# Float64 weight decoding without its maximum and mask, and a new step list, in a fused linear-attention and two-layer mixture kernel

## The chip, the cores and the metric

The kernel runs on one core of one Trainium2 chip. The metric is the time of one execution in microseconds (us), as the device reports it. Engines are named as in the profile: PE is TensorE's matmuls and PEld its weight loads, DVE is VectorE, ACT is ScalarE, POOL is GpSimd, SP is SyncE, which issues the DMAs.

## The reference

Three blocks follow each other. The first is a linear attention with a decaying state over 768 positions (4 batches, 8 heads of 48). The second is a feed-forward layer `g = h * cos(h)` with `h = x @ w_in`, whose two matrices `w_in` (384 x 2048) and `w_out` (2048 x 384) arrive as float64. The third is a soft mixture of eight experts.

```python
for t in range(S):
    cur = np.einsum('bhd,bhe->bhde', u[None] * kt, vt)
    y[:, :, t] = np.einsum('bhd,bhde->bhe', rt, state + cur)
    state = wt[:, :, :, None] * state + np.einsum('bhd,bhe->bhde', kt, vt)
...
h = x @ w_in
g = h * np.cos(h)
return (g @ w_out).astype(np.float32)
...
logits = x @ phi          # softmax over tokens (dispatch) and over slots (combine)
slot_out[e] = np.maximum(slot_input[e] @ w1[e], 0.0) @ w2[e]
return (c @ slot_out).astype(np.float32)
```

## The kernel before

The 3072 tokens are cut into 24 blocks of 128 (j, or t in the feed-forward part). Every piece of work is a named step, and a string `HEAD` of about 1900 step names is the whole schedule: the steps are emitted in that order, and each engine executes its own instructions in that order. There is no other scheduler; an engine that waits holds up everything behind it in its own list.

The steps that matter here:

- Attention for block j: loads `lw lk lr lv lz`, transposes on TensorE `wT rT kT kN`, two scans on VectorE `scan` (line 149) and `sp` (line 157), `ks` (line 184, it reads the transposed k out of PSUM), `L`, `mask`, `z`, `st`, `bo`; `ru` and `D` are POOL's (lines 162, 163, 207); matmuls `A U y`; the result x is split into a high and a low part by `xh` and `xl`.
- Decoding the float64 weights, 256 columns of `w_in` (i.0 to i.7) or 256 rows of `w_out` (o.0 to o.7) at a time. `raw` loads the pairs of 32-bit words. `abs` (line 325, ScalarE) reads the high word as a float32 and takes its absolute value. `mx` (line 329, VectorE) takes the maximum with the smallest high word that still fits float32. `d1` (line 333) shifts left by 3 and masks, `d2a` (line 338) brings sign and top exponent bit in from the high word, `d2b` (line 346) brings three bits in from the low word. For w_in, `whi`, `wn`, `wc` then split the result into a high and a low part on ScalarE and TensorE; for w_out, `oT`, `oc`, `om`, `pc`, `pT`, `ps` multiply it with phi ahead of time. The raw tiles of most blocks have two buffers, so a `raw` waits for the `d2b` of two blocks before.
- Feed-forward for block t and quarter q of the columns: `h.t.q` is nine matmuls (lines 434 to 436), then `turns` (ScalarE), `rest` (VectorE), `cos` (ScalarE), `mul` (VectorE), `gT` (TensorE), `gc` (ScalarE), `l` (TensorE).
- Once per pair of blocks g the logits are summed up: `sum lc max exp xt xr xd dT dc ltok E es`, between TensorE, VectorE and ScalarE.

The decoding is spread over the first quarter of the list, between attention blocks 0 to 5 and feed-forward blocks 0 and 1. Block i.0 is decoded in two halves, so 16 blocks make 17 of each decode step.

Of the kernel before, what the change touches and what calls it, by code (L numbers as in the profile page):

```python
# [21 lines left out]
def rwkv_moe_kernel(ctx: ExitStack, tc: tile.TileContext, r, k, v, w, u, w_in, w_out, phi, w1, w2, cst, out):  # L22
    nc = tc.nc
# [323 lines left out]

    def e_d2s(x, n, hf=None):

        lo = part(raw_t[x, n, hf], hf)[..., 0]  # L350
        nc.vector.tensor_scalar(out=lo, in0=lo, scalar1=29, scalar2=None, op0=ALU.logical_shift_right)

    def e_d2p(x, n, hf=None):
        ai, dst = cut(x, n, hf)
        nc.gpsimd.tensor_tensor(out=dst, in0=part(raw_t[x, n, hf], hf)[..., 0], in1=ai, op=ALU.add)
# [529 lines left out]
d2b.o.3 lz.1 mx.o.1 wc.0.1 abs.o.0 U.1 rz.1.0 st.1.0 d1.o.1 kT.2 mx.o.0 d2a.o.1 z.1.1 raw.i.4 d2b.o.1 ks.2 d1.o.0 y.0 lw.3 st.1.1 abs.o.2 rz.1.1 sr.2
d2a.o.0 lk.3 mx.o.2 kN.2 ksn.2 d2b.o.0 d1.o.2 oT.3 z.2.0 oT.0 d2a.o.2 abs.i.1 lr.2 mx.i.1 oc.0 d2b.o.2 y.1 oc.3 xh.0 d1.i.1 oT.2 xl.0 xh.1 abs.i.4
xl.1 oT.4 oc.2 oT.5 oc.4 lr.3 oc.5 ru.2 wT.3 oT.1 sp.2 wf.3 rT.2 oc.1 lv.2 d2a.i.1 mx.i.4 lw.4 d2b.i.1 U.2 L.2 st.2.0 d1.i.4 raw.i.3 whi.1 scan.3 bo.2
om.0 wn.1.0 d2a.i.4 rz.2.0 wn.1.1 wc.1.0 z.2.1 wc.1.1 lw.5 abs.i.3 bs.2 d2b.i.4 whi.4 A.2 raw.i.6 h.0.0 D.2 ru.3 mx.i.3 lr.4 kT.3 sr.3 d1.i.3 st.2.1
d2a.i.3 pc.0 mask.2 turns.0.0 d2b.i.3 raw.i.5 wn.4.0 whi.3 sp.3 ks.3 wc.4.0 wn.4.1 rest.0.0 lz.2 abs.i.6 wc.4.1 wT.4 mx.i.6 wf.4 z.3.0 cos.0.0 oT.6
d1.i.6 oc.6 scan.4 wn.3.0 wn.3.1 wc.3.0 oT.7 abs.i.5 d2a.i.6 rT.3 h.1.0 sr.4 d2b.i.6 oc.7 wc.3.1 mx.i.5 L.3 d1.i.5 whi.6 turns.1.0 mul.0.0 wn.6.1  # L890
rest.1.0 wn.6.0 wT.5 wc.6.1 gT.0.0 raw.i.7 rz.3.0 pT.0 d2a.i.5 h.0.1 rz.2.1 lr.5 sp.4 ps.0 lk.4 lv.3 A.3 wc.6.0 bo.3 y.2 abs.i.7 bs.3 D.3 gc.0.0 wf.5
d2b.i.5 whi.5 raw.o.4 turns.0.1 lw.6 om.1 mx.i.7 mask.3 xh.2 kN.3 wn.5.0 cos.1.0 ksn.3 rest.0.1 cos.0.1 xl.2 pc.1 d1.i.7 mul.1.0 d2a.i.7 wc.5.0 wn.5.1
kT.4 wc.5.1 abs.o.4 U.3 ks.4 d2b.i.7 mx.o.4 h.0.2 turns.0.2 lw.7 st.3.0 lk.5 mul.0.1 whi.7 d1.o.4 kN.4 h.1.1 ru.4 wn.7.0 gT.0.1 z.3.1 rest.0.2 lz.3
lv.4 rz.3.1 ksn.4 wn.7.1 turns.1.1 d2a.o.4 scan.5 st.3.1 cos.0.2 d2b.o.4 y.3 wc.7.0 raw.o.5 abs.o.5 wc.7.1 bo.4 mul.0.2 rest.1.1 l.0.0 mx.o.5 rT.4
pT.1 cos.1.1 gc.0.1 h.0.3 ps.1 oT.9 L.4 raw.o.6 d1.o.5 gT.0.2 mul.1.1 lv.5 lr.6 lk.6 bs.4 d2a.o.5 turns.0.3 rest.0.3 xh.3 oT.8 abs.o.6 gc.0.2 oc.8
h.1.2 d2b.o.5 oT.11 mx.o.6 z.4.0 oc.9 xl.3 cos.0.3 turns.1.2 oT.10 oc.11 d1.o.6 l.0.1 mul.0.3 A.4 oc.10 raw.o.7 U.4 lz.4 d2a.o.6 om.2 st.4.0 d2b.o.6
abs.o.7 kT.5 gT.0.3 gc.0.3 rest.1.2 z.4.1 ru.5 h.1.3 ks.5 mx.o.7 pc.2 pT.2 st.4.1 cos.1.2 ps.2 oT.12 d1.o.7 sr.5 mul.1.2 bo.5 gT.1.1 ru.6 rT.5 sp.5
d2a.o.7 oc.12 l.0.2 L.5 bs.5 wT.6 rz.4.1 d2b.o.7 close D.4 wf.6 h.2.0 gc.1.1 kN.5 mask.4 gT.1.0 turns.1.3 ksn.5 gc.1.0 oT.13 A.5 oc.13 oT.15 rest.1.3
gT.1.2 oT.14 z.5.0 l.1.0 rz.4.0 D.5 oc.15 turns.2.0 mask.5 oc.14 y.4 lk.7 l.1.1 om.3 cos.1.3 xh.4 mul.1.3 rest.2.0 lz.5 U.5 xl.4 h.2.1 pc.3 st.5.0
lw.8 gc.1.2 z.5.1 cos.2.0 mul.2.0 scan.6 turns.2.1 gT.1.3 pT.3 sr.6 rest.2.1 bo.6 ps.3 rz.5.1 gc.1.3 h.2.2 kT.6 gT.2.0 l.1.2 l.0.3 l.1.3 cos.2.1 sp.6  # L900
rT.6 lr.7 ks.6 turns.2.2 wT.7 gc.2.0 sum.0 st.5.1 rest.2.2 lc.0 mul.2.1 bs.6 cos.2.2 L.6 kN.6 lv.7 lk.8 rz.5.0 h.2.3 ksn.6 A.6 mul.2.2 D.6 wf.7 max.0
exp.0 lv.6 U.6 z.6.0 turns.2.3 gT.2.1 scan.7 gc.2.1 xt.0 rest.2.3 st.6.0 lr.8 z.6.1 st.6.1 xr.0 h.3.0 sr.7 cos.2.3 lv.8 kT.7 turns.3.0 mul.2.3 ru.7
gT.2.2 gc.2.2 xd.0 bo.7 ks.7 rT.7 bs.7 dT.0 ltok.0 h.3.2 lz.6 rest.3.0 kN.7 l.2.0 dc.0 cos.3.0 ru.8 ksn.7 lr.9 sp.7 mul.3.0 rz.6.1 lw.9 E.0.0 y.5
mask.6 turns.3.2 xh.5 h.3.1 gT.2.3 turns.3.1 wT.8 l.2.1 L.7 bo.8 l.2.2 rest.3.2 E.0.1 lk.9 xl.5 wf.8 cos.3.2 rest.3.1 gc.2.3 mul.3.2 rz.6.0 bs.8 A.7
cos.3.1 es.0 gT.3.0 h.3.3 gc.3.0 scan.8 sr.8 kT.8 turns.3.3 lk.10 mul.3.1 gT.3.2 l.2.3 rest.3.3 l.3.0 y.6 D.7 gc.3.2 h.4.1 gT.3.1 cos.3.3 turns.4.1
mask.7 ks.8 xh.6 rT.8 z.7.0 mul.3.3 sp.8 xl.6 wT.9 rest.4.1 h.4.0 rz.7.0 wf.9 L.8 gc.3.1 turns.4.0 gT.3.3 U.7 D.8 cos.4.1 lz.7 lw.10 st.7.0 z.7.1 A.8
mul.4.1 gc.3.3 l.3.1 rest.4.0 lr.10 l.3.2 rz.7.1 cos.4.0 st.7.1 scan.9 l.3.3 y.7 sum.1 mask.8 h.4.2 mul.4.0 turns.4.2 sr.9 rest.4.2 gT.4.1 sp.9 ru.10
lc.1 cos.4.2 max.1 kN.8 mul.4.2 lw.11 gc.4.1 ksn.8 h.5.0 wT.10 bo.10 exp.1 xt.1 gT.4.0 wf.10 kT.9 h.4.3 bs.10 ks.9 xr.1 xd.1 xh.7 dT.1 turns.5.0 kN.9
gc.4.0 gT.4.2 rest.5.0 dc.1 turns.4.3 xl.7 U.8 cos.5.0 gc.4.2 l.4.0 ltok.1 z.8.0 rest.4.3 mul.5.0 l.4.1 st.8.0 E.1.0 z.8.1 ru.9 h.5.1 st.8.1 rT.9
cos.4.3 mul.4.3 scan.10 turns.5.1 gT.4.3 rest.5.1 h.5.2 L.9 rz.8.1 z.9.0 ksn.9 cos.5.1 gc.4.3 lw.12 lz.8 turns.5.2 lv.9 mul.5.1 A.9 U.9 rest.5.2  # L910
cos.5.2 bo.9 lv.10 h.6.1 sr.10 st.9.0 rz.8.0 gT.5.1 mul.5.2 wT.11 turns.6.1 gc.5.1 h.5.3 sp.10 lz.9 rest.6.1 z.9.1 st.9.1 kT.10 bs.9 wf.11 D.9 gT.5.0
turns.5.3 E.1.1 cos.6.1 l.4.2 y.8 gc.5.0 xh.8 l.5.0 scan.11 l.4.3 rest.5.3 mask.9 rT.10 mul.6.1 ks.10 sr.11 cos.5.3 mul.5.3 gT.5.2 kN.10 h.6.0 gc.5.2
# [109 lines left out]
```

## Time and profile before

| what | value |
|---|---|
| time, median of 3 runs | 530.23 us (529.28 to 530.65) |
| the profiled execution's own time | 529.87 us |
| its span, first to last instruction | 528.2 us |
| PE busy | 486.2 us (92%) |
| DVE busy | 434.1 us (82%) |
| ACT busy | 319.4 us (60%) |
| POOL busy | 100.0 us (19%) |

The profiled execution lies within the range of the timed ones. Its span is 1.67 us shorter than its time; that difference lies outside the first and last instruction. A busy share is an average over the whole span: the first 64 us, the middle and the last 50 us have different limits.

### The profile page before, as it was taken

The numbers are of one execution on the slowest core, as the hardware profiler recorded it, in microseconds if no ns is written. First come the engines' busy times: TensorE is split into PE (matmuls) and PEld (weight loads), VectorE is DVE, ScalarE is ACT, GpSimd is POOL, SyncE is SP. The second block draws the span as 40 slices with busy tenths as digits, with TensorE's granted clock in tenths as the row PEclk, the third lists the DMA queues.
The fourth block names the chain that finished last, engine by engine and source line by source line (L and its number), as shares of the span: only waits on it lengthen the run. The fifth ranks groups of instructions, "written<-read, shape, count | busy, mean of one in ns | idle before, by whom it ended". The sixth has DMA issues, their size and how long they took to land.

```text
span 528.2 us, 15546 instructions
## 1 busy us (share of the span) xinstructions
PE 486.2 (92%) x6515; PEld 381.2 (72%) x6515; DVE 434.1 (82%) x826; ACT 319.4 (60%) x703; POOL 100.0 (19%) x127
## 2 busy tenths in 40 slices
...
GB/s 184 331 208 70 190 143 203 178 58 70 54 77 64 13 80 88 62 47 59 78 23 56 76 31 51 58 91 82 57 2 47 337 378 7 118 269 325 402 175 267
DMA packets 146325, 67.47 MB, mean 128 GB/s; under 512 B 127184, under 2 KB 134352, under 8 KB 146256
## 3 DMA queue, kind: packets, MB, share of 16 engines
...
## 4 chain that ended last, share of the span: by engine, by line
PE 70%; DVE 18%; ACT 4%; DMA 4%; issue 2%; SPq 0%; ACTq 0%; DVEq 0%
PE h L434 11%; PE h L436 10%; PE h L435 10%; PE gT L468 7%; PE l L483 4%; PE E L579 4%; PE y L267 4%; PE A L193 3%; PE U L239 2%; PE hps L767 2%; DVE lt L214 2%; PE so L807 2%; PE wT L134 2%; PE kT L134 2%; PE kN L200 1%
## 5 line engine op out<-in xcount | busy, mean ns | idle before, releaser
L434 PE MATMUL h<-wu,x 128*128 128x512 f32 x288 | 121.6, 422 | 0.8 <-DVE g L461 0.8
L436 PE MATMUL h<-wu,x 128*128 128x512 f32 x288 | 113.1, 393 | 0.0
L435 PE MATMUL h<-wu,x 128*128 128x512 f32 x288 | 112.5, 391 | 0.0
L449 ACT ACTIVATE g<-h 128x512 int32<-128x512 f32 (+1 forms) x96 | 57.1, 596 | 54.4 <-PE h L436 47.2
L457 ACT ACTIVATE g<-g,half_pi 128x512 f32<-128x512 f32 (+1 forms) x97 | 69.0, 718 | 22.7 <-DVE g L453 21.5
L461 DVE TENSOR_TENSOR g<-g,h 128x512 f32<-128x512 f32 x96 | 64.5, 675 | 17.2 <-ACT g L457 16.9
L453 DVE SCALAR_TENSOR_TENSOR g<-g,h 128x512 f32<-128x512 int32 (+1 forms) x96 | 64.6, 675 | 12.2 <-ACT g L449 11.7
L207 POOL TENSOR_SCALAR_AFFINE_SELECT lt<-bo 64x512 f32<-64x512 f32 x48 | 35.3, 736 | 179.6 <-ACT bo L230 121.3
L434 PEld LDWEIGHTS h<-wu,x 128*128 128x128 f32 x288 | 54.2, 188 | 15.0 <-DVE g L461 4.1
L474 ACT COPY gt<-gT 128x512 f32<-128x512 f32 x89 | 51.8, 583 | 20.0 <-PE gT L468 15.6
L436 PEld LDWEIGHTS h<-wu,x 128*128 128x128 f32 x288 | 54.0, 188 | 12.4
L435 PEld LDWEIGHTS h<-wu,x 128*128 128x128 f32 x288 | 54.4, 189 | 8.7
L468 PE MATMUL gT<-cs,g 128*128 128x128 f32 x384 | 57.7, 275 | 0.6 <-ACT gt L474 0.5
L162 POOL TENSOR_TENSOR ru<-rn,u_b 128x384 f32<-128x384 f32 x24 | 28.9, 1203 | 137.5 <-DVE bo L225 70.3
L468 PEld LDWEIGHTS gT<-cs,g 128*128 128x128 f32 x384 | 44.7, 141 | 8.3 <-issue 2.2
L214 DVE COPY_PREDICATED lt<-cs,A 64x512 f32<-64x512 uint32 x48 | 35.4, 737 | 3.2 <-PE A L193 1.8
L149 DVE TENSOR_TENSOR_SCAN qt<-wf,one_b 128x520 f32<-128x520 f32 x24 | 30.9, 1289 | 5.5 <-ACT wf L144 5.3
L253 ACT COPY rzs<-z 64x192 f32<-64x192 f32 x96 | 33.4, 348 | 1.8 <-DVE z L248 0.9
L483 PE MATMUL l<-gt,p_sb 128*32 128x128 f32 x768 | 31.7, 277 | 1.9 <-ACT gt L474 1.6
L178 DVE TENSOR_TENSOR lt<-rT,pt 64x512 f32<-64x512 f32 x48 | 32.8, 684 | 0.5
L157 DVE TENSOR_TENSOR_SCAN pt<-wf,ini_f 128x520 f32<-128x520 f32 x24 | 30.6, 1274 | 0.1
L267 PEld LDWEIGHTS y<-lt,rzs 128*32 128x32 f32 x1536 | 24.7, 112 | 6.3 <-issue 2.4
...
## 6 DMA issues: line engine op xcount, KB each, us to landing
...
```

The lines of the kernel that those rows point to most:

```text
L214: nc.vector.copy_predicated(out=lt[j % 2][h, a], mask=mask[h].bitcast(U32).unsqueeze(1).to_broadcast([64, NS, C]), data=ps[h])
L267: nc.tensor.matmul(ps[m:m + 32, o, c * C:(c + 1) * C], lhsT=rz[:, c, p, a, 32 * b:32 * b + 32], rhs=L[:, a, 2 * p + c, :], start=m not in ...
L434: nc.tensor.matmul(half[:, f], lhsT=xh[:, c, :], rhs=wh, start=(c == 0), stop=False)
L435: nc.tensor.matmul(half[:, f], lhsT=xl[:, c, :], rhs=wh, start=False, stop=False)
L436: nc.tensor.matmul(half[:, f], lhsT=xh[:, c, :], rhs=wl, start=False, stop=(c == KD - 1))
L449: nc.scalar.activation(gt.bitcast(I32), hp, AF.Copy, bias=0.25, scale=1.0 / TWO_PI)
L453: nc.vector.scalar_tensor_tensor(out=gt, in0=gt.bitcast(I32), scalar=-TWO_PI, in1=hp, op0=ALU.mult, op1=ALU.add)
L457: nc.scalar.activation(gt, gt, AF.Sin, bias=half_pi[:, 0:1])
L461: nc.vector.tensor_tensor(out=gt, in0=gt, in1=hp, op=ALU.mult)
L468: nc.tensor.transpose(ps[:, m * 128:(m + 1) * 128], gt[:, m * 128:(m + 1) * 128], ident)
L474: (nc.vector.tensor_copy if n >= ATT and n % 8 in (1, 2, 5) else nc.scalar.copy)(gt_t[t, q], pend.pop(("gT", t, q)))
L483: nc.tensor.matmul(lps_t[g][32 * m:32 * m + 32, o:o + TB], lhsT=p_sb[:, 4 * q + m, :], rhs=gt[:, m * 128:(m + 1) * 128], start=first, stop ...
```

## The change

ScalarE's `abs` gets a scale of 2^-112, which lowers the exponent so far that what follows needs no maximum and no mask. The `mx` step is gone, `d1` only shifts, `d2a` takes the sign bit alone from the high word. Three steps that no list used go as well. `HEAD` is replaced by another list of the same steps without the 17 `mx`.

```diff
-        nc.scalar.activation(part(a_t[x, n], hf), part(raw_t[x, n, hf], hf)[..., 1].bitcast(F32), AF.Abs)
-
-    def e_mx(x, n, hf=None, eng=nc.vector):
-        a = part(a_t[x, n], hf)
-        eng.tensor_scalar(out=a, in0=a, scalar1=TINY_HI_F, scalar2=None, op0=ALU.max)
-
-    def e_d1(x, n, hf=None):
+        nc.scalar.activation(part(a_t[x, n], hf), part(raw_t[x, n, hf], hf)[..., 1].bitcast(F32), AF.Abs, scale=2.0 ** -112)
+
+    def e_shift(x, n, hf=None):
         ai = part(a_t[x, n].bitcast(I32), hf)
-        nc.vector.tensor_scalar(out=ai, in0=ai, scalar1=3, scalar2=0x3FFFFFF8, op0=ALU.logical_shift_left, op1=ALU.bitwise_and)
-
-    def e_d2a(x, n, hf=None):
+        nc.vector.tensor_scalar(out=ai, in0=ai, scalar1=3, scalar2=None, op0=ALU.logical_shift_left)
+
+    def e_sign(x, n, hf=None):
 
         hi, ai = part(raw_t[x, n, hf], hf)[..., 1], part(a_t[x, n].bitcast(I32), hf)
-        nc.vector.scalar_tensor_tensor(out=ai, in0=hi, scalar=-0x40000000, in1=ai, op0=ALU.bitwise_and, op1=ALU.bitwise_or)
+        nc.vector.scalar_tensor_tensor(out=ai, in0=hi, scalar=-0x80000000, in1=ai, op0=ALU.bitwise_and, op1=ALU.bitwise_or)
...
-raw.i.0.1 d2a.i.2 d2b.i.2 L.0 bo.0 bs.0 whi.2 U.0 D.0 scan.1 st.0.0 A.0 rz.0.0 sr.1 raw.i.0.0 kT.1 z.0.1 abs.i.0.1 mask.0 abs.i.0.0 ks.1 ru.1 wn.2.1
...
-TINY_HI_F = 2.0 ** (0x38000000 // 0x800000 - 127)
```

What the new list does is best seen where VectorE comes to `ks.3`, about 63 us into the program of before. Before, VectorE's rows there are these (ai_644 is block i.3, ai_722 is block i.6, ks_711 is `ks.3`, pt_709 is `sp.3`):

```order
L329 TENSOR_SCALAR ai_644<-ai_644 128x768
L153 RECIPROCAL ini_f<-qt_613 128x8
L333 TENSOR_SCALAR ai_644<-ai_644 128x768
L256 TENSOR_TENSOR st_state<-U_1_589,z_1_640 128x192
L338 SCALAR_TENSOR_TENSOR ai_644<-rawi_610,ai_644 128x768
L214 COPY_PREDICATED lt_125<-cs,A_651 64x512 x2
L346 SCALAR_TENSOR_TENSOR ai_644<-rawi_610,ai_644 128x768
L157 SCALAR_TENSOR_TENSOR pt_709<-wf,ini_f 128x520
L184 TENSOR_TENSOR ks_711<-kT_687,qt_613 128x512
```

In the change the same place on VectorE reads as follows (ai_661 is block i.3, ai_712 is block i.6, ks_717 is `ks.3`, pt_724 is `sp.3`; lines 334 and 342 are the old 338 and 346, and line 329 is now the shift):

```order
L214 COPY_PREDICATED lt_125<-cs,A_644 64x512 x2
L334 SCALAR_TENSOR_TENSOR ai_661<-rawi_601,ai_661 128x768
L342 SCALAR_TENSOR_TENSOR ai_661<-rawi_601,ai_661 128x768
L153 RECIPROCAL ini_f<-qt_642 128x8
L184 TENSOR_TENSOR ks_717<-kT_694,qt_642 128x512
L157 SCALAR_TENSOR_TENSOR pt_724<-wf,ini_f 128x520
L329 TENSOR_SCALAR ai_712<-ai_712 128x768
```

The maximum of block i.3 is gone, and the scan `sp.3` has moved from ahead of `ks.3` to behind it.

The second place is the start of SP's list. Before, the loads come in this order (wn_121, kn_119 and rn_117 are w, k and r of block 0, wn_122 is w of block 1, rawi_156 is weight block i.2):

```order
L117 DMA wn_121<-in_w_dram 128x8x48
L310 DMA rawi_156<-in_moe_w_in_dram 128x3x512
L117 DMA kn_119<-in_k_dram 128x8x48
L662 DMA u_b<-in_u_dram 128x384
L663 DMA phi_sb<-in_moe_phi_dram 128x3x32
L117 DMA rn_117<-in_r_dram 128x8x48
L117 DMA wn_122<-in_w_dram 128x8x48
```

In the change SP's list begins so (rawi_157 is block i.2, rawi_175 the first half of block i.0):

```order
L117 DMA wn_121<-in_w_dram 128x8x48
L117 DMA kn_119<-in_k_dram 128x8x48
L310 DMA rawi_157<-in_moe_w_in_dram 128x3x512
L117 DMA wn_122<-in_w_dram 128x8x48
L310 DMA rawi_175<-in_moe_w_in_dram 128x3x256
L117 DMA rn_117<-in_r_dram 128x8x48
L649 DMA u_b<-in_u_dram 128x384
```

The k of block 0 now goes ahead of the first weight block, and r of block 0 behind the first half of i.0.

## Rows read from the trace of the kernel before

**Rows 1.** First line of the page.

```profile
span 528.2 us, 15546 instructions
```

**Rows 2.** Busy time in five stretches: start:end, length, engines, PE clock, DMA share, GB/s.

```profile
6.32:28.00 21.68, 12.63 (x102) 8.32 (x102) 20.59 (x31) 7.89 (x18) 7.95 (x8) 0.85 1.07 277
28.00:64.10 36.10, 25.48 (x346) 18.73 (x345) 34.96 (x54) 19.53 (x38) 8.46 (x6) 0.78 0.65 146
64.10:114.10 50.00, 48.34 (x585) 38.46 (x589) 47.43 (x77) 36.85 (x79) 12.31 (x12) 0.95 0.72 162
114.10:476.60 362.50, 358.16 (x4858) 287.24 (x4846) 311.65 (x618) 235.96 (x523) 61.30 (x70) 1.00 0.38 89
476.60:528.20 51.60, 40.46 (x637) 27.77 (x637) 19.24 (x48) 16.81 (x45) 6.67 (x10) 0.95 0.82 289
```

**Rows 3.** The chain that ended last, share of the span by engine.

```profile
PE 70%; DVE 18%; ACT 4%; DMA 4%; issue 2%; SPq 0%; ACTq 0%; DVEq 0%
```

**Rows 4.** That chain in order of time, 20 to 70 us: start, length, what.

```profile
20.94 1.08 DVE ai L329 x2
...
34.53 0.47 DVE ao L329
...
50.52 4.71 DMA rawi<-in_moe_w_in_dram
...
55.31 0.94 ACT ai L325
...
56.27 0.56 DVE ai L329
...
62.40 1.15 DVE pt L157
...
64.19 1.12 PE wT L134 x4
...
69.14 0.46 PE woT L388 x3
```

**Rows 5.** VectorE's decode groups to 115 us, shapes apart: count, busy us, mean ns.

```profile
L338 DVE SCALAR_TENSOR_TENSOR ai<-rawi,ai 128x768 int32<-128x768 int32 x7 | 8.6, 1225 | 0.0
...
L329 DVE TENSOR_SCALAR ao<-ao 128x768 f32<-128x768 f32 x8 | 4.4, 552 | 1.3 <-ACT ao L325 1.3
L333 DVE TENSOR_SCALAR ao<-ao 128x768 int32<-128x768 int32 x8 | 4.4, 548 | 0.0
L329 DVE TENSOR_SCALAR ai<-ai 128x768 f32<-128x768 f32 x7 | 4.3, 619 | 1.0 <-ACT ai L325 0.9
...
L329 DVE TENSOR_SCALAR ai<-ai 128x384 f32<-128x384 f32 x2 | 1.2, 612 | 0.0
```

**Rows 6.** VectorE's timeline: start, length, line, what.

```profile
9.11 0.56 DVE L329 TENSOR_SCALAR ai<-ai 128x768 f32<-128x768 f32 x1
...
28.00 0.56 DVE L329 TENSOR_SCALAR ao<-ao 128x768 f32<-128x768 f32 x1
28.48 0.55 DVE L346 SCALAR_TENSOR_TENSOR ai<-rawi,ai 128x384 int32<-128x384 int32 x1
...
57.94 2.10 DVE L338 SCALAR_TENSOR_TENSOR ai<-rawi,ai 128x768 int32<-128x768 int32 x1
```

**Rows 7.** POOL's timeline around 58 us.

```profile
58.24 0.99 POOL L162 TENSOR_TENSOR ru<-rn,u_b 128x384 f32<-128x384 f32 x1
59.31 1.60 POOL L163 TENSOR_TENSOR ru<-ru,kn 128x384 f32<-128x384 f32 x1
```

**Rows 8.** Two ScalarE groups to 115 us: with scale and bias, and a plain copy.

```profile
L449 ACT ACTIVATE g<-h 128x512 int32<-128x512 f32 x9 | 5.4, 601 | 3.9 <-PE h L436 3.9
L382 ACT CAST wu<-wl 128x512 fp32r<-128x512 f32 x8 | 4.7, 585 | 9.4 <-PE wl L377 9.4
```

**Rows 9.** The chain in order of time, one hand-off of the logits.

```profile
459.59 0.45 PE lc L496 x2
...
465.32 1.07 PE E L579 x8
```

More of the change, by code (lines that the diff above doesn't have):

```diff
@@ L346, in e_d2b @@
         nc.vector.scalar_tensor_tensor(out=dst, in0=part(raw_t[x, n, hf], hf)[..., 0], scalar=29, in1=ai, op0=ALU.logical_shift_right, op1=ALU.bitwise_or)
[L348 to L355, printed above, removed]
     def win(n):
@@ L885 @@
[L885 to L912, printed above, removed]
@@ L969 @@
-rest.23.3.0 l.22.0 mul.23.3.1 gc.23.0 l.22.1 gT.22.2 rest.23.1 cos.23.1 cos.23.3.0 we.6 gc.22.2 gT.23.2 l.23.0 l.22.2 mul.23.1 gc.23.2 l.22.3 gT.23.1
-mul.23.3.0 gc.23.1 gT.23.3 l.23.1 gc.23.3 l.23.2 l.23.3 sum.11 lc.11 we.7 E.10.1 tab max.11 quart.11 exp.11 dT.11 es.10 dc.11 E.11.1 E.11.0 esl.11.1
-ltok.11 esl.11.0
+lw.0 lk.0 raw.i.2 z.0.0 wT.0 lw.1 kT.0 wf.0 scan.0 raw.i.0.0 abs.i.2 ks.0 sr.0 sp.0 d1.i.2 d2a.i.2 wT.1 lr.0 misc kN.0 ru.0 wf.1 scan.1 ksn.0 d2b.i.2
+rT.0 lv.0 abs.i.0.0 lr.1 raw.i.0.1 lk.1 abs.i.0.1 sr.1 U.0 L.0 d1.i.0.0 raw.o.2 lw.2 rT.1 raw.o.0 lv.1 bo.0 lk.2 bs.0 D.0 sp.1 lz.0 st.0.0 d2a.i.0.0
@@ new lines @@
+z.0.1 A.0 L.1 raw.i.1 mask.0 st.0.1 whi.2 rz.0.1 wn.2.0 ru.1 d1.i.0.1 kT.1 lr.2 wn.2.1 z.1.0 wc.2.0 d2a.i.0.1 d2b.i.0.0 abs.o.3 rz.0.0 d2b.i.0.1 bo.1
+wT.2 lz.1 ks.1 d1.o.3 wf.2 kN.1 lw.3 ksn.1 bs.1 d2a.o.3 wc.2.1 raw.i.4 D.1 scan.2 A.1 d2b.o.3 whi.0 mask.1 wn.0.0 abs.o.1 lv.2 d1.o.1 U.1 d2a.o.1
+wc.0.0 st.1.0 wn.0.1 d2b.o.1 z.1.1 abs.o.0 abs.o.2 rz.1.0 y.0 d1.o.0 st.1.1 wc.0.1 d2a.o.0 sr.2 oT.2 ru.2 oc.2 oT.3 xh.0 oc.3 d2b.o.0 rz.1.1 kT.2
+d1.o.2 xl.0 oT.1 ks.2 lv.3 oT.0 sp.2 y.1 abs.i.1 oc.1 d2a.o.2 d1.i.1 oc.0 kN.2 d2b.o.2 wT.3 om.0 wf.3 xh.1 d2a.i.1 xl.1 oT.4 ksn.2 oT.5 oc.4 U.2
@@ new lines @@
+d2b.i.1 oc.5 z.2.0 raw.i.3 st.2.0 lw.5 whi.1 abs.i.4 z.2.1 bo.2 rT.2 bs.2 st.2.1 L.2 wn.1.0 wc.1.0 lz.3 d1.i.4 wn.1.1 wc.1.1 d2a.i.4 rz.2.0 oT.7
+scan.3 A.2 abs.i.3 d2b.i.4 d1.i.3 lk.3 D.2 mask.2 d2a.i.3 raw.i.6 h.0.0 oc.7 whi.4 wn.4.1 d2b.i.3 rz.2.1 wc.4.1 kT.3 turns.0.0 wn.4.0 lw.4 whi.3 lr.3
+pc.0 ru.3 abs.i.6 sr.3 raw.i.5 ks.3 wc.4.0 oT.6 sp.3 oc.6 d1.i.6 wn.3.0 rest.0.0 wc.3.0 wn.3.1 lk.4 d2a.i.6 rT.3 wT.4 d2b.i.6 wc.3.1 L.3 z.3.0 wf.4
+whi.6 cos.0.0 h.1.0 abs.i.5 scan.4 pT.0 raw.i.7 turns.1.0 wn.6.1 d1.i.5 wc.6.1 wn.6.0 bo.3 wT.5 mul.0.0 wc.6.0 sr.4 d2a.i.5 h.0.1 abs.i.7 d2b.i.5 sp.4
@@ new lines @@
+whi.5 bs.3 lz.2 A.3 ps.0 turns.0.1 lr.4 rz.3.0 y.2 wf.5 D.3 xh.2 om.1 rest.1.0 d1.i.7 kN.3 cos.1.0 mask.3 ksn.3 wn.5.0 rest.0.1 cos.0.1 wc.5.0 wn.5.1
+mul.1.0 raw.o.4 gT.0.0 wc.5.1 d2a.i.7 kT.4 xl.2 lz.4 d2b.i.7 mul.0.1 abs.o.4 whi.7 U.3 pc.1 ks.4 ru.4 raw.o.5 st.3.0 h.0.2 wn.7.0 d1.o.4 turns.0.2
+z.3.1 gc.0.0 d2a.o.4 wn.7.1 rest.0.2 wc.7.1 st.3.1 h.1.1 rT.4 gT.0.1 cos.0.2 abs.o.5 wc.7.0 scan.5 turns.1.1 d2b.o.4 bo.4 lw.6 oT.8 oc.8 mul.0.2
+rest.1.1 sr.5 kN.4 d1.o.5 h.0.3 bs.4 cos.1.1 L.4 mul.1.1 pT.1 rz.3.1 d2a.o.5 lk.5 ksn.4 gc.0.1 y.3 turns.0.3 h.1.2 rest.0.3 oT.9 xh.3 ps.1 cos.0.3
@@ new lines @@
+raw.o.7 lv.4 d2b.o.5 oT.11 gT.0.2 z.4.0 turns.1.2 oc.11 lr.5 oc.9 D.4 xl.3 oT.10 oc.10 A.4 rest.1.2 U.4 mul.0.3 l.0.0 sp.5 l.0.1 st.4.0 mask.4 abs.o.7
+lw.7 lr.6 z.4.1 om.2 cos.1.2 pc.2 gc.0.2 raw.o.6 mul.1.2 abs.o.6 h.2.0 ru.5 gT.0.3 rz.4.1 rT.5 gc.0.3 pT.2 d1.o.6 h.1.3 ps.2 rz.4.0 d1.o.7 st.4.1 wT.6
+d2a.o.6 d2b.o.6 turns.1.3 wf.6 L.5 kT.5 gT.1.1 lz.5 ks.5 d2a.o.7 gc.1.1 lr.7 lw.8 lv.5 oT.12 oT.13 turns.2.0 kN.5 oc.12 d2b.o.7 close rest.1.3 lk.6
+bo.5 ksn.5 z.5.0 gT.1.0 l.0.2 gc.1.0 oc.13 A.5 oT.14 gT.1.2 oT.15 bs.5 scan.6 oc.14 D.5 l.1.0 l.1.1 oc.15 cos.1.3 gc.1.2 mul.1.3 ru.6 y.4 rest.2.0
```

132 lines of the change are left out of this document (72 added, 60 removed).

## The prediction

> **What bounds the kernel now.** I read the chain that ended last first. By engine it is 70% TensorE and 18% VectorE [rows 3], so there are two bounds, and the question is where each holds. The busy times by stretch tell that [rows 2]. From 6.32 to 28.00 us VectorE is busy 20.59 of 21.68 us, and from 28.00 to 64.10 us it is busy 34.96 of 36.10; TensorE has only 12.63 and 25.48 there. From 64.10 us on it turns round: TensorE is busy 48.34 of 50.00 us, then 358.16 of 362.50, then 40.46 of 51.60 in the tail. So VectorE sets the pace for the first 64 us, and after that a gain can only come from what TensorE still waits: 1.66 us to 114.10, 4.34 us in the middle, and a tail that the change does not touch by its own steps.
>
> The chain in order of time shows the hand-over [rows 4]. It runs through VectorE, with two maxima at 20.94, others at 34.53 and 56.27, and the scan `sp.3` at 62.40. At 64.19 TensorE starts the transpose `wT.4`: it needs a PSUM buffer that `ks.3` on VectorE gives back. From there TensorE runs almost without a gap. The end of `ks.3` is thus the moment that the change has to bring forward.
>
> **What goes.** Up to `ks.3` I compared the two step lists. VectorE's steps of the new list are exactly those of the old one without ten maxima (i.2, both halves of i.0, o.3, o.1, o.0, o.2, i.1, i.4, i.3) and without `sp.3`, which now stands behind `ks.3`. Nothing is added ahead of it.
>
> A maximum of a whole block takes 0.552 us on average in the o blocks, 0.619 in the i blocks; the two halves are 0.612 each [rows 5]. What one costs on the path is less, because consecutive VectorE instructions overlap a little: the one at 28.00 us takes 0.56, and the next starts at 28.48 [rows 6]. The chain shows the same 0.47 to 0.56 for one and 1.08 for the two halves [rows 4]. So:
> - the two halves 1.08;
> - i.2 at 9.11 us 0.56 [rows 6], i.3 0.56 [rows 4];
> - the other six 0.47 each, 2.82;
> - sum for ten maxima 5.02 us;
> - `sp.3` behind `ks.3`: 1.15 [rows 4].
>
> That is 6.17 us, call it 6.2. `sp.3` is only moved, but at its new place VectorE's lead is no longer what TensorE waits for: what follows `ks.3` on TensorE first are splits and transposes of things that are ready.
>
> The other seven maxima lie behind 64 us, where TensorE is the bound. I price them at nothing. The work that hides them is TensorE's 48.34 busy us [rows 2]. If that cover were thinner than it looks, they would give back the 1.66 us that TensorE idles there, no more, since nothing is left to wait for beyond that.
>
> One transpose of w_out, `oT.7`, goes from behind `wT.4` (0.46 us at 69.14 [rows 4]) to a place ahead of it, where TensorE has idle time. I take 0.5.
>
> **What the changed instructions cost.** The shift without the mask stays one instruction over the same elements; its neighbours with one operation (the maximum, 552 ns) and with two (the shift and mask, 548) take the same [rows 5], so I price it at nothing. `d2a` changes only a constant. The scale in `abs`: line 449 has a scale and a bias and takes 601 ns for 512 columns, a plain copy of the same size 585 [rows 8]. At worst the 16 ns come on top of each of 17 `abs`, 0.3 us on an engine that is busy 19.53 of 36.10 us [rows 2]: nothing.
>
> **What the new order costs.** Three places could eat the gain.
> - *Reloading the raw tiles.* A `raw` load waits for the `d2b` two blocks before. The load takes 4.71 us, `abs` 0.94, and only then does VectorE go on [rows 4]; the loop is closed at 56.27, so it takes about 5.8 us from the issue at 50.52. I added up VectorE's steps that the new list puts into each of the eight such loops, by their durations in the timeline: seven hold 5.6 us or more and one (i.4 to i.6) 5.5. I expect waits of 0.3 us at most there, behind `ks.3`. From below: if every loop fell short by 0.5 us, 4 us of the gain would go.
> - *Loads at the start.* In the first stretch the DMA engines are full (share 1.07 [rows 2]). Block 0's k moves ahead of block i.2, and r of block 0 moves behind half a weight block more, which is 128 x 3 x 256 words of 4 bytes, 393 KB; at 277 GB/s that is 1.4 us later. VectorE comes to `L.0`, which needs r, after two scans and the decode of i.2, so I price it at 0, with 1.4 us as the other end.
> - *Meetings with GpSimd.* At 57.94 a `d2a` takes 2.10 us, against a mean of 1.225 for its kind [rows 5, 6], while POOL runs two multiplications from 58.24 to 60.91 [rows 7]. So one meeting costs VectorE 0.9 us or more. POOL is busy 7.95 + 8.46 = 16.4 us in the two stretches [rows 2], and the new list puts these steps beside other VectorE work. I keep as many meetings as before, and allow three more or fewer: 2.7 us either way.
>
> The Trainium skill ("SBUF — State Buffer", section "SBUF: two separate sides") says of this that VectorE and GpSimd share one pair of SBUF ports, which is locked for a whole instruction, for VectorE operations with two SBUF inputs and for those that run in a two-port mode. The 2.10 us of row group 6 agree. By that rule the maxima, too, held the lock, so that without them GpSimd would meet VectorE less often; with no meetings at all up to 64 us the sum below would come out lower by the few us that they now cost, which is the direction of my second rival.
>
> **The sum.** 6.2 + 0.5 = 6.7 us less span: 528.2 - 6.7 = 521.5 us [rows 1]. Outside the span lie 1.67 us, which gives 523.2 us against the profiled execution's 529.87. That one is 0.36 us faster than the median of 530.23, so the change against the median is about 7 us, or 1.3%. A difference under 0.3% (1.6 us) can't be told from none here.
>
> **The rivals.**
>
> *Gain half eaten (0.17).* The first 64 us stay VectorE's, but reload waits (up to 4 us), the late r (1.4 us) or three more meetings (2.7 us) take the place of the maxima. For it: DMA is full at the start, and the slack of the loops is only some tenths. Against it: before, the loop of i.3 held 5.7 us of VectorE steps and VectorE did not stall for it. It gives 525.5 to 531 us.
>
> *More than the sum (0.13).* VectorE's head start also removes TensorE's 1.66 us up to 114.10 and a part of its 4.34 us in the middle [rows 2], and there are fewer meetings. The bound is 6.7 + 1.66 + 2.7, about 11 us: 519 us, and 518 if the middle gives something. For it: the chain still runs through 18% VectorE [rows 3]. Against it: both engines' lists change in the middle as well, and TensorE has hardly a gap to close.
>
> *The middle loses (0.12; the one on the other side).* From 114.10 to 476.60 the whole list is new, and TensorE has 4.34 us of idle time in 362.50 [rows 2]; there is little to win there and much to lose. The place is the hand-off of the logits, which happens for 11 pairs of blocks there. `lc` on TensorE at 459.59 is followed by maximum, exponential, division and transpose on VectorE and ScalarE, and TensorE comes to `E` at 465.32 [rows 9], 5.7 us later. In the new list TensorE's own work between `lc` and `dT` is less: by my count over the list the median goes from 7.3 to 5.5 us. If TensorE has to wait 0.8 us at each of the 11, that is 8.8 us and the sign turns; it needs more than 6.7 + 1.6 = 8.3 us to be slower. For it: the shorter cover. Against it: VectorE is ahead by the maxima when the middle begins. It gives 529 to 534 us.
>
> *The forecast (0.58):* 520.5 to 525.5 us.
>
> That the change does not do what it says is no rival of weight: the maxima are gone from VectorE's list.
>
> **How the numbers follow.** The predicted time is the forecast's, 523.2. Below 519 I leave about 0.07 (the far end of the second rival), above 529.5 about 0.12 (the third and the end of the first), so the range is 519 to 529.5. Faster by over 0.3%, under 528.6: the forecast 0.58, the second rival 0.13, of the first 0.11, sum 0.82. Within 0.3%, 528.6 to 531.8: 0.05 of the first and 0.03 of the third, 0.08. Slower: 0.10.
>
> **What would show it.** In the changed kernel's profile VectorE should stay above 94% busy up to `ks.3`, no VectorE line should have 17 one-operation instructions beside the shift, and `ks.3` should end at about 57.5 to 58.5 us, with TensorE all but gapless from there (before, its successor starts at 64.19). `abs` should take what it took. From that point to the end the kernel should need the same time as before, 528.2 - 64.2 = 464.0 us, give or take 2. I am wrong if VectorE idles in the first 60 us for a raw tile, if its two-input decode steps grow longer than before, or if TensorE's idle time between 114 and 476 us grows by several us.

## The result and the profile after

The changed kernel takes 516.77 us (median of 4 runs, 516.31 to 517.41), the kernel before, on the same chip, 530.44 (529.28 to 531.05). The ratio is 0.9746, with a 95% interval of 0.9725 to 0.9767: 13.7 us less, twice what I forecast (7 us), and below the low end of my range.

The profiled execution took 517.14 us with a span of 515.4 us. Its busy times in five stretches, cut at the same or neighbouring steps as [rows 2] (columns as there: start:end, length, then PE, PEld, DVE, ACT and POOL busy, PE clock, DMA share, GB/s):

```profile
6.65:26.50 19.85, 12.45 (x99) 9.12 (x98) 18.93 (x29) 6.54 (x13) 6.25 (x6) 1.00 1.14 291
26.50:57.86 31.36, 23.51 (x352) 16.18 (x351) 30.33 (x45) 21.05 (x44) 6.99 (x6) 0.95 0.78 169
57.86:105.35 47.49, 45.56 (x571) 36.11 (x575) 45.95 (x71) 36.85 (x78) 12.11 (x11) 1.00 0.77 173
105.35:464.51 359.16, 357.12 (x4858) 288.07 (x4850) 311.53 (x618) 234.94 (x523) 64.90 (x74) 1.00 0.39 89
464.51:515.40 50.89, 40.84 (x637) 27.42 (x637) 19.24 (x48) 16.94 (x45) 6.68 (x10) 0.95 0.83 293
```

The reader is to see two things. Up to 57.86 us VectorE is as full as before, 49.26 of 51.21 us (96%): the time of the maxima went out of the stretch and not into idle time. And behind it TensorE idles 1.93 and 2.04 us where it idled 1.66 and 4.34 before [rows 2].

VectorE's timeline at the hand-over (start, length, line, what):

```profile
56.23 0.96 DVE L342 SCALAR_TENSOR_TENSOR ai<-rawi,ai 128x768 int32<-128x768 int32 x1
57.10 0.20 DVE L153 RECIPROCAL ini_f<-qt 128x8 f32<-128x8 f32 x1
57.22 0.64 DVE L184 TENSOR_TENSOR ks<-kT,qt 128x512 f32<-128x512 f32 x1
57.78 1.23 DVE L157 TENSOR_TENSOR_SCAN pt<-wf,ini_f 128x520 f32<-128x520 f32 x1
59.34 0.56 DVE L329 TENSOR_SCALAR ai<-ai 128x768 int32<-128x768 int32 x1 [0.33 <-ACT ai L325]
```

`ks.3` ends at 57.86 us instead of 64.13, 6.27 us earlier; I had forecast 6.17. The unforecast part of the gain must lie behind this point. To see where, I cut both programs at events that they share: the end of `ks.3`, the first sum of logits `lc.0`, the last but one, `lc.10`, and the end of the program. Of before:

```profile
64.13:123.90 59.77, 58.14 (x760) 46.77 (x761) 57.10 (x92) 44.00 (x95) 12.33 (x13) 0.96 0.64 142
123.90:459.43 335.53, 331.81 (x4518) 266.30 (x4517) 290.30 (x573) 217.42 (x482) 61.27 (x70) 1.00 0.37 82
459.43:528.20 68.77, 57.01 (x790) 40.41 (x788) 30.89 (x77) 28.17 (x69) 6.67 (x10) 0.96 0.78 276
```

and of the changed kernel:

```profile
57.86:117.26 59.40, 57.47 (x764) 46.13 (x764) 56.76 (x89) 45.26 (x98) 16.59 (x17) 1.00 0.68 150
117.26:447.26 330.00, 328.52 (x4507) 265.41 (x4506) 288.76 (x572) 215.13 (x478) 60.42 (x68) 1.00 0.38 83
447.26:515.40 68.14, 57.53 (x790) 40.05 (x788) 31.20 (x76) 28.34 (x69) 6.68 (x10) 0.96 0.79 279
```

The three lengths fall by 0.37, 5.53 and 0.63 us, together 6.53; with the 6.27 ahead of them that is 12.8, the whole difference of the spans. The 5.53 are not all gain of the middle: from the number of steps that each list has ahead of `lc.0`, and TensorE's durations for them, I count about 2.1 us of TensorE's work that the new list does before `lc.0` and the old one behind it. So the part up to `lc.0` gives about 8.7 us, the middle about 3.4 and the tail 0.6.

### The profile page after: what moved, and what is told of

Its sections match the earlier page's. It is cut to its first block, busy times and chain, and to the rows that moved or that the text cites. A ratio compares the mean times of both kernels' runs of the same rounds, so it can differ in the third digit from the quotient of the medians.

```text
span 515.4 us, 15516 instructions
## 1 busy us (share of the span) xinstructions
PE 481.4 (93%) x6515; PEld 378.3 (73%) x6515; DVE 426.2 (83%) x809; ACT 318.7 (62%) x703; POOL 100.2 (19%) x127
## 4 chain that ended last, share of the span: by engine, by line
PE 53%; DVE 7%; ACT 3%; issue 1%
PE h L421 9%; PE h L423 8%; PE h L422 8%; PE gT L455 6%; PE l L470 3%; PE E L566 3%; PE A L193 2%; PE hps L754 2%; PE so L794 2%; PE y L267 2%; PE U L239 1%; DVE g L440 1%; PE o L827 1%; PE rT L134 1%; PE kT L134 1%; DVE lt L214 1%
## 5 line engine op out<-in xcount | busy, mean ns | idle before, releaser
L448 DVE TENSOR_TENSOR g<-g,h 128x512 f32<-128x512 f32 (+1 forms) x96 | 64.7, 675 | 13.3 <-ACT g L444 12.3
L207 POOL TENSOR_SCALAR_AFFINE_SELECT lt<-bo 64x512 f32<-64x512 f32 x48 | 37.3, 778 | 159.4 <-ACT bo L230 89.6
L455 PE MATMUL gT<-cs,g 128*128 128x128 f32 x384 | 57.5, 275 | 0.2
L162 POOL TENSOR_TENSOR ru<-rn,u_b 128x384 f32<-128x384 f32 x24 | 26.2, 1092 | 133.8 <-DMA rn<-in_r_dram 82.9
L193 PE MATMUL A<-lt,ks 64*64 64x64 f32 x768 | 28.0, 224 | 3.0 <-DVE st_state L256 1.6
```

Of the source, the lines that this page charges most:

```text
L193: nc.tensor.matmul(ps[64 - 64 * a:128 - 64 * a, s, :], lhsT=ks[k, s, :], rhs=L[k, a, s, :], start=True, stop=True)
L448: nc.vector.tensor_tensor(out=gt, in0=gt, in1=hp, op=ALU.mult)
L455: nc.tensor.transpose(ps[:, m * 128:(m + 1) * 128], gt[:, m * 128:(m + 1) * 128], ident)
```

## The experiments

All kernels were timed beside the kernel before, in four sets; its median over the sets was 528.7 to 530.4 us. Medians are compared as they stand, since the part from `lc.0` to `lc.10` in the old order takes 335.5 us in the profiles of three of the sets (335.53 in the kernel before, 335.54 and 335.58 in `old_list_no_max` and `old_max_seven` below). As the kernel before itself moves by 1.7 us between sets, differences under about 2 us between kernels of different sets are not read from their times alone. Two theories stood at first: that the gain is VectorE's, and any list would pass it on (theory 1), or that the new list brings a part of its own, in the middle above all (theory 2).

**The two halves of the change apart.** `old_list_no_max` has the new decode code and the old list without its seventeen `mx`:

```diff
-lw.0 lk.0 raw.i.2 z.0.0 wT.0 lw.1 kT.0 wf.0 scan.0 ...
+lw.0 raw.i.2 lk.0 misc lr.0 lw.1 z.0.0 wT.0 wf.0 lv.0 kT.0 abs.i.2 ...
```

> The new decode code with the OLD step list, from which only the 17 maxima are struck out. Theory 1 (the gain is VectorE's: 17 instructions less, and the list only closes the gaps): most of the 13.7 us, so 517 to 520 us. Theory 2 (the new list brings its own part, in the middle above all): only the prologue's part, about 5 to 6 us, so 524 to 525 us. If the maxima behind 64 us are worth nothing, as the prediction said, ks.3 ends at about 59 us (10 maxima less, sp.3 still ahead of it) and nothing is gained after it.

`new_list_with_max` has the old decode code and the new list, with `mx` ahead of each `d1`:

```diff
-... scan.0 ks.0 sr.0 sp.0 d1.i.2 d2a.i.2 ...
+... scan.0 ks.0 sr.0 sp.0 mx.i.2 d1.i.2 d2a.i.2 ...
```

> The OLD decode code with the NEW step list, with a maximum put back right ahead of each shift. Theory 1: nearly all the gain is lost, 527 to 531 us. Theory 2: the list alone is worth 5 to 8 us, so 522 to 525 us; the middle from the first logits on is as quick as in the changed kernel.

Measured: 523.97 us (ratio 0.9897, 0.9879 to 0.9916) and 528.44 us (0.9976, 0.9964 to 0.9988). Each part alone gives little, 5.3 and 0.9 us, and both together 13.7:

| median, us | old list | new list |
|---|---|---|
| with the maxima | 529.3 to 530.4 | 528.4 |
| without | 524.0 | 516.8 |

Theory 1 had the second number right and theory 2 the first, so neither will do. The same maxima are worth 5.3 us in the old list and 11.7 in the new one. I had expected `ks.3` to end at about 59 us in `old_list_no_max`; it ended at 57.30. From there to the end the profiled execution took 464.4 us, against 464.0 in the kernel before, so in the old order nothing is gained behind `ks.3`, as the forecast had it. The middle tells more, from `lc.0` to `lc.10` of `old_list_no_max` and then of `new_list_with_max`:

```profile
117.71:453.25 335.54, 331.71 (x4518) 266.21 (x4516) 290.21 (x573) 217.41 (x482) 61.24 (x70) 1.00 0.38 82
```

```profile
129.79:459.89 330.10, 329.05 (x4508) 265.56 (x4507) 290.15 (x572) 214.58 (x478) 62.45 (x68) 1.00 0.38 83
```

The old order needs 335.5 us for it with the maxima or without, the new one 330.0 or 330.1. So the middle's gain is the order's alone; no head start of VectorE enters into it. What `new_list_with_max` loses, it loses ahead of `lc.0`, which comes 12.5 us later than in the changed kernel.

**The list cut at `lc.0`.** `new_then_old` has the new list up to `lc.0` and the remaining steps in the old order, `old_then_new` the reverse; both with the new decode code.

```diff
 HEAD, new_then_old:
 ... cos.2.1 mul.2.1 turns.2.2 L.6 rest.2.2 gc.2.0 kT.6 h.2.3 lk.7 lc.0
-bs.6 ks.6 cos.2.2 turns.2.3 sr.7 ...
+(the old list without what stands above)
```

> The changed kernel whose list follows the new order up to the first logits (step lc.0, at 117 us in the changed kernel) and then takes the remaining steps in the old order. Theory 1 (the middle's 3.4 us come from VectorE being ahead): as quick as the changed kernel, 516 to 518 us. Theory 2 (they come from the new order of the middle): 520 to 521 us.

> The old list without maxima up to the first logits (lc.0), then the remaining steps in the new order. Theory 1: equal to the old list without maxima (within 1 us). Theory 2: quicker than the old list without maxima by the middle's 3 to 4 us, about 520 to 521 us.

Measured: 522.34 us (0.9868, 0.9848 to 0.9888) and 522.08 us (0.9864, 0.9845 to 0.9884). Both are over 1 us slower than theory 2's 520 to 521 us and fit theory 1 less still: each half of the list alone gives less than the whole. In `old_then_new` the seam costs something: TensorE waits 2.2 us there for one of VectorE's products (`h` for `mul`), where its longest such wait in the changed kernel is 0.5. `new_then_old` is the cleaner one: the same program as the changed kernel up to `lc.0`, and 5.6 us slower by the medians. In the two profiles 4.0 us of it lie behind `lc.0` (402.1 against 398.1 us), 3.8 of them ahead of `lc.10`, and 0.7 us ahead of `lc.0`, where the programs are the same. What TensorE waited for between 117 and 460 us, first in `new_then_old`, then in the changed kernel (total us, times, longest):

```profile
PE l L470 <- ACT gt L461: 1.6, 1, 1.6
PE h L421 <- DVE g L448: 0.8, 2, 0.4
PE gT L455 <- ACT gt L461: 0.5, 1, 0.5
PE E L566 <- ACT dt L547: 0.5, 2, 0.3
PE E L566 <- DVE ltok L553: 0.3, 1, 0.3
...
```

```profile
PE h L421 <- DVE g L448: 0.5, 1, 0.5
PE E L566 <- ACT g L436: 0.3, 1, 0.3
PE A L193 <- DVE x L285: 0.3, 1, 0.3
PE rT L134 <- DVE st_state L256: 0.3, 1, 0.3
```

The first three of the first list stand in the profiles of the kernel before, `old_list_no_max` and `old_max_seven` too, with the same lengths to 0.1 us (1.6 for `l`, 0.7 or 0.8 for `h`, 0.5 for `gT`). These waits belong to the written order: they came back in each of the four profiled kernels that have it.

**One wait of the old middle taken away.** The longest of them, in `new_then_old`, on VectorE, ScalarE and TensorE:

```profile
193.09 1.23 DVE L149 TENSOR_TENSOR_SCAN qt<-wf,one_b 128x520 f32<-128x520 f32 x1
...
194.35 0.47 DVE L553 COPY ltok<-dT 64x64 f32<-64x64 f32 x2
194.90 0.42 ACT L547 COPY dt<-dT 64x64 f32<-64x64 f32 x2 [2.29 <-DVE ltok L553]
195.35 0.59 ACT L461 COPY gt<-gT 128x512 f32<-128x512 f32 x1
...
195.99 0.43 PE L470 MATMUL l<-gt,p_sb 128*32 128x128 f32 x8 [1.57 <-ACT gt L461]
```

TensorE's `l.6.0` needs the copy `gc.6.0`; that stands on ScalarE behind `dc.2`, which waits for `ltok.2`, which stands on VectorE behind the scan `scan.12`. `old_middle_mended` moves two steps:

```diff
-turns.7.1 dT.2 scan.12 ltok.2 gT.6.0 ru.11 y.9 dc.2 sr.12
+turns.7.1 dT.2 ltok.2 dc.2 scan.12 gT.6.0 ru.11 y.9 sr.12
```

> The kernel of new_then_old (new list up to lc.0, old order behind it) with two steps moved: ltok.2 and dc.2 stand ahead of scan.12 instead of behind it. In new_then_old TensorE waits 1.57 us at 195.99 us for one of ScalarE's copies (gc.6.0), which stands behind dc.2, which waits for ltok.2, which stands behind a scan of 1.22 us on VectorE. If what the new middle order gains are such waits, this one wait falls under 0.3 us and the span to 1.3 to 1.5 us less than new_then_old's 520.1: 520.5 to 521.3 us as a median against 522.34. If the middle's gain is not in its waits (TensorE fills the time again by some other wait right behind): 522 to 522.6 us.

Measured: 520.82 us (520.62 to 520.95; 0.9848, 0.983 to 0.9867), 1.5 us less than `new_then_old`, and its span is 518.9 against 520.1. The row of `l.6.0` is now

```profile
194.53 0.43 PE L470 MATMUL l<-gt,p_sb 128*32 128x128 f32 x8 [0.42 <-ACT gt L461]
```

It comes 1.46 us earlier, but 0.68 of that had been gained by `lc.0` already (117.31 against 117.99 us), up to which the two programs are the same. The wait is 0.42, not under 0.3 as I had said; 1.15 us of it are gone. What that is worth shows from `lc.2` to `lc.3`, where the wait lies, first in `new_then_old`, then here:

```profile
186.82:221.32 34.50, 32.64 (x466) 25.79 (x464) 30.03 (x62) 21.54 (x50) 8.94 (x10) 1.00 0.33 59
```

```profile
186.23:220.11 33.88, 32.64 (x466) 25.79 (x464) 30.32 (x63) 21.66 (x50) 8.94 (x10) 1.00 0.32 60
```

The stretch is 0.62 us shorter; between the other sums of logits the two kernels agree within 0.05 us. The other half came back beside it: TensorE now waits 0.30 us for a product of VectorE two steps later, and 0.52 instead of 0.24 us at the transpose ahead. So the time fell into the range that I had named, but only 0.6 of the 1.5 us are the move's: a wait in the middle does cost time, but taking it away gave only about half of its length.

**The maxima ahead of `ks.3` and behind it.** My forecast priced the ten ahead at 5.0 us and the seven behind at nothing. Three kernels have the new decode code and a maximum against zero put back in some of the decodes:

```diff
+    def e_mx(x, n, hf=None):
+        a = part(a_t[x, n], hf)
+        nc.vector.tensor_scalar(out=a, in0=a, scalar1=0.0, scalar2=None, op0=ALU.max)
...
-... ks.3 wc.4.0 oT.6 sp.3 oc.6 d1.i.6 ...
+... ks.3 wc.4.0 oT.6 sp.3 oc.6 mx.i.6 d1.i.6 ...
```

> The changed kernel with a maximum (against zero, which changes no value) put back ahead of the shift in the ten decodes ahead of ks.3 only. Theory A (in the new order VectorE stays the bound past ks.3, until the last decode, so that each maximum costs its own time wherever it stands; the ten cost 5 to 6 us, the seven 6 to 7): 521.8 to 523.0 us, with ks.3 near 63 us and ks.5 about 6 us later than in the changed kernel. Theory B (the seven behind ks.3 are hidden under TensorE, as I had priced them, and the loss of 11.7 us with all seventeen comes from the ten ahead): 526 to 528.5 us.

> The changed kernel with a maximum (against zero) put back in the seven decodes behind ks.3 only (i.6, i.5, i.7, o.4 to o.7). Theory A: ks.3 stays at 57 to 58 us, ks.5 comes 6 to 7 us later than in the changed kernel, and the time is 521.8 to 524 us. Theory B: 516.5 to 518 us, the time of the changed kernel or at most the microsecond that TensorE idles there.

> The new decode code in the old step list, with the maximum (against zero) left in the seven decodes behind ks.3 and gone from the ten ahead of it. Beside it stands the old list without any maximum, 523.97 us. Theory A: in the old order TensorE is the bound behind ks.3 and the seven cost nothing or nearly so: 523.5 to 525 us. If the seven cost their VectorE time in this order as well, 527.5 us or more, and then the difference between the two lists is not in where VectorE is the bound.

Measured: `new_max_ten` 523.01 us (0.9884, 0.9864 to 0.9904), `new_max_seven` 523.03 (0.9883, 0.9863 to 0.9902), `old_max_seven` 524.74 (six runs, 522.70 to 525.87; 0.9909, 0.9888 to 0.9931). In the new list the ten cost 6.2 us and the seven 6.3 (5.5 each against `two_op_shift` below, which is timed in the same set and differs from the changed kernel by nothing that shows); in the old list the seven cost 0.8 over the 523.97 without them, which the spread of those runs does not tell from nothing. The row of `ks.5` (start, length) shows the place, in the changed kernel, in `new_max_seven`, and in the old list without and with the seven:

```profile
100.36 0.69 DVE L184 TENSOR_TENSOR ks<-kT,qt 128x512 f32<-128x512 f32 x1
```

```profile
57.20 0.64 DVE L184 TENSOR_TENSOR ks<-kT,qt 128x512 f32<-128x512 f32 x1
...
106.45 0.69 DVE L184 TENSOR_TENSOR ks<-kT,qt 128x512 f32<-128x512 f32 x1
```

```profile
96.94 0.68 DVE L184 TENSOR_TENSOR ks<-kT,qt 128x512 f32<-128x512 f32 x1
```

```profile
96.42 0.68 DVE L184 TENSOR_TENSOR ks<-kT,qt 128x512 f32<-128x512 f32 x1
```

With the seven, `ks.3` stays at 57.2 and `ks.5` is 6.1 us late in the new list; in the old list, where six of the seven stand ahead of it, it is not late at all (the profiled execution of `old_max_seven` is the fastest of its six, 522.70 us). Theory A holds in the main: in the new order VectorE is the bound until the last decode near 100 us, in the old one only until `ks.3`. The busy times agree. Between `ks.3` and `lc.0` the old list without maxima leaves VectorE idle 6.5 us (53.88 busy of 60.41, the first row of the last section; 4.4 in the other execution there), which the seven fit into; the changed kernel leaves it 2.64 (56.76 of 59.40, above).

That each maximum costs its own time is only a part of it. The seven take 3.8 us in `new_max_seven`, but VectorE's busy time from `ks.3` to `lc.0` grows by 6.8 us (63.56 against 56.76). Other instructions got longer beside GpSimd's, two above all, a shift and the scan `sp.5` (timelines of VectorE and GpSimd in `new_max_seven`):

```profile
73.46 1.87 DVE L333 TENSOR_SCALAR ai<-ai 128x768 int32<-128x768 int32 x1
...
73.91 1.00 POOL L162 TENSOR_TENSOR ru<-rn,u_b 128x384 f32<-128x384 f32 x1
...
96.14 1.01 POOL L163 TENSOR_TENSOR ru<-ru,kn 128x384 f32<-128x384 f32 x1
96.21 2.03 DVE L157 TENSOR_TENSOR_SCAN pt<-wf,ini_f 128x520 f32<-128x520 f32 x1
```

In the changed kernel they take 0.58 and 1.23 us; in `new_list_with_max` 1.87 and 2.00. So about 4 of the 6.3 us are the maxima's own, and most of the rest goes with meetings with GpSimd that lengthen VectorE's instructions in the new order with the maxima and not without them.

**The mask.** `two_op_shift` is the changed kernel with a second operation in the shift again.

```diff
-scalar1=3, scalar2=None, op0=ALU.logical_shift_left)
+scalar1=3, scalar2=0x7FFFFFF8, op0=ALU.logical_shift_left, op1=ALU.bitwise_and)
```

> The changed kernel with the shift followed again by a mask (of 31 bits, which changes no value), in the same instruction. I priced the mask that goes at nothing: 516.0 to 517.6 us, and 548 ns for a whole block's shift. The rival, that an instruction with one operation is the quicker one and part of the gain is its own: 0.1 us for each of seventeen would be 1.5 to 2 us more, 518.3 us or above.

Measured: 517.52 us (517.15 to 517.99; 0.9778, 0.9759 to 0.9796); the shift has a median of 551 ns in `w_in` blocks and 552 in `w_out` blocks, against 554 and 557 with one operation. A mask in the same instruction costs nothing that shows: the instruction's own duration says so, and the 0.75 us between the medians of two sets are not read.

**`sp.3` put back ahead of `ks.3`.**

```diff
-raw.i.5 ks.3 wc.4.0 oT.6 sp.3 oc.6
+raw.i.5 sp.3 ks.3 wc.4.0 oT.6 oc.6
```

> The changed kernel with sp.3 put back ahead of ks.3. My forecast took 1.15 us for this move. If ks.3 is what TensorE waits for: 517.6 to 518.3 us. If VectorE is the bound until the last decode, as the runs with maxima say, the order of two of its steps far ahead of that counts for nothing: ks.3 ends 1.15 us later and the time is 516.3 to 517.4 us, that of the changed kernel.

Measured: 517.04 us (516.62 to 518.10; 0.978, 0.976 to 0.9801), the changed kernel's time as far as two sets can tell. `ks.3` did not even end later in its profile (57.53 us), so that part of my expectation failed; the same program up to there varies by up to 1.3 us between executions (57.38 to 58.67 in three kernels that share it). `lc.0` comes at 116.29 us, against 117.26 in the changed kernel. So the move of `sp.3` gives nothing by itself that these executions show.

**One VectorE instruction less.** If VectorE still is the bound, taking more off it should pay. `sign_by_scalar` leaves the sign to ScalarE. Its decoded weights are not the reference's; it is read for its time alone.

```diff
-        nc.scalar.activation(part(a_t[x, n], hf), part(raw_t[x, n, hf], hf)[..., 1].bitcast(F32), AF.Abs, scale=2.0 ** -112)
+        nc.scalar.activation(part(a_t[x, n], hf), part(raw_t[x, n, hf], hf)[..., 1].bitcast(F32), AF.Copy, scale=2.0 ** -112)
+        hi = part(raw_t[x, n, hf], hf)[..., 1].bitcast(F32)
+        nc.scalar.activation(hi, hi, AF.Copy, bias=-0.0, scale=0.0)
...
-        nc.vector.scalar_tensor_tensor(out=ai, in0=hi, scalar=-0x80000000, in1=ai, op0=ALU.bitwise_and, op1=ALU.bitwise_or)
+        nc.vector.scalar_tensor_tensor(out=ai, in0=ai, scalar=3, in1=hi, op0=ALU.logical_shift_left, op1=ALU.bitwise_or)
```

> The changed kernel with one VectorE instruction less for each block: ScalarE copies the high words with the scale (sign and all, no Abs), and then multiplies the raw high words by zero, which leaves the sign bit; VectorE shifts and joins the two in one instruction, where it used two. The list is the changed one without the seventeen shifts. If VectorE is still the bound up to the last decode, 17 instructions of 0.55 us (9 us) are off it, while TensorE has only 1.9 us of idle time between ks.3 and 105 us and some 20 us ahead of ks.3: I expect ks.3 some 4 us earlier and 511 to 514 us. Rival: ScalarE, with 17 instructions of 0.9 us more, becomes the one that VectorE waits for in the decode, and the time stays within 2 us of the changed kernel's, 515 to 519 us.

Measured: 518.19 us (516.60 to 519.67; 0.9799, 0.9773 to 0.9825): the rival. Up to 57.86 us VectorE has less to do than in the changed kernel, 44.80 us instead of 49.26, and ScalarE more, 35.78 instead of 27.59:

```profile
6.65:57.86 51.21, 36.69 (x451) 26.26 (x451) 44.80 (x64) 35.78 (x67) 12.99 (x12) 0.97 0.90 215
```

Yet `ks.3` starts at 56.68, only 0.54 us earlier, which is within the spread of executions named above. The 4.5 us taken off VectorE became idle time. Its longest new wait, in the timelines of ScalarE and VectorE:

```profile
25.34 0.90 ACT L325 ACTIVATE ao<-rawo 128x768 f32<-128x768 f32 x1 [2.11 <-PE wl L361]
...
26.27 0.90 ACT L327 ACTIVATE rawo<-rawo 128x768 f32<-128x768 f32 x1
...
27.20 0.96 DVE L332 SCALAR_TENSOR_TENSOR ao<-ao,rawo 128x768 int32<-128x768 int32 x1 [2.08 <-PE kN L200]
```

The page names TensorE's `kN` as what ended the 2.08 us, but VectorE's instruction at 27.20 reads `rawo` from ScalarE's added one (L327), which ends at 27.17: that is what it waits for, and it in turn stands behind a ScalarE instruction that waited 2.11 us for the split of another block.

An instruction of 0.55 us left VectorE and one of 0.92 entered ScalarE in the same chain from load to decoded block. So "VectorE is the bound" is true for what is added to it, and no longer true for what is taken off and put on ScalarE; what less work on VectorE alone would give, no run shows.

## Why the prediction was wrong

**What held.** VectorE set the pace up to `ks.3`, stayed above 94% busy (96%), and `ks.3` ended at 57.86, within the 57.5 to 58.5 that I gave. `abs` takes what it took: medians of 902 and 928 ns, against 910 and 910 before. The mask is free. No reload loop and no late load of r shows as a wait of VectorE up to there.

**Right by a wrong split, and in part by luck.** The 6.17 us up to `ks.3` were 5.02 for ten maxima and 1.15 for `sp.3`. Put back alone, the ten move the start of `ks.3` by 5.63 us (62.85 against 57.22), and `sp.3` moves it by nothing that can be told from the spread. That 6.27 came out so close to 6.17 is luck besides: the old list without maxima reached the end of `ks.3` at 57.30 and at 59.30 us in two executions of the same program. I have no run on `oT.7` (0.5 us).

**The step that failed** is "from that point to the end the kernel should need the same time as before, 464.0 us, give or take 2". It needs 515.4 - 57.9 = 457.5. The old list without maxima does need 464.4, so the step was right for the old order and failed for the new one. Of the 6.5 us about 2.5 lie ahead of `lc.0` (0.37 shorter, with about 2.1 of TensorE's work done early), 3.4 in the middle and 0.6 in the tail; where the tail's come from no run shows. Under the step lie two prices of nothing:

- *The seven maxima behind 64 us.* I read the cover from the old order, TensorE's 48.34 busy us [rows 2], and bounded the gain by TensorE's 1.66 idle us. For the old order that is right: the seven cost 0.8 us there, within the spread. But the new list puts more of TensorE's work ahead of `lc.0` in the same time, and in that order VectorE has too little time left for them and for the meetings with GpSimd that they bring: with the seven in place the whole gain would have been 6.3 us less. The bound was right for the kernel that I had a trace of, and wrong for the kernel that I had to forecast.
- *The middle.* I saw TensorE's 4.34 us of idle time there and thought only of what the new order could add to it. It removes 2.24 us of it between `lc.0` and `lc.10` (3.72 idle before, 1.48 after, by the rows above), and as many matmuls take TensorE less time: 328.52 busy us for 4507 against 329.81 for 4507 in `new_then_old`, another 1.3 us. Its row, from `lc.0` to `lc.10`:

```profile
117.99:451.76 333.77, 329.81 (x4507) 264.58 (x4506) 287.88 (x571) 216.04 (x478) 59.98 (x68) 1.00 0.38 82
```

Why the matmuls pack better in the new order I have not tested.

**The rivals.** "More than the sum" had the right direction, but its main mechanism, a head start of VectorE that helps the middle, is refuted: the middle is as long with the maxima as without. What it said of fewer meetings holds behind `ks.3` in the new order, as `new_max_seven` shows. "The middle loses" is refuted at its own place. In the changed kernel TensorE has less work between `lc` and `dT`, as I had counted, and still waits at no hand-off for the exponentials; between 117 and 460 us the only wait at an `E` in its list is 0.3 us. Nor did the gain get eaten by meetings with GpSimd. The `d2a` of the `w_in` blocks fell from a mean of 1225 ns [rows 5] to 944:

```profile
L334 DVE SCALAR_TENSOR_TENSOR ai<-rawi,ai 128x768 int32<-128x768 int32 x7 | 6.6, 944 | 0.1
...
L329 DVE TENSOR_SCALAR ao<-ao 128x768 int32<-128x768 int32 x8 | 5.1, 648 | 1.3 <-ACT ao L325 1.2
```

but the shift of the `w_out` blocks rose from 548 to 648. That is one of the eight: it took 1.35 us at 38.66, while GpSimd's `ru` of 38.01 took 1.60. The Trainium skill ("SBUF — State Buffer", section "SBUF: two separate sides") says that GpSimd's operations and those of VectorE with two SBUF inputs or in a two-port mode shut each other out of shared ports. The rows fit meetings that moved from one decode instruction to another. That they become fewer without the maxima, as I had read the rule, these two rows do not show; behind `ks.3` in the new order the seven did bring more of them.
